# Waiting at the end for all output stores, also for those known to have landed

## The chip, the cores and the metric

The kernel runs on one core of one Trainium2 chip. The metric is the device time of one execution in microseconds (us). The median of three runs of the kernel before is 99.98 us (99.91 to 100.34).

## The reference

The kernel computes one block of linear attention in bf16, with B = 1, S = 2048 rows, D = 640 columns and 32 heads of 20 columns each:

```python
qkv = (x @ wqkv) -> q, k, v, each [B, 32, S, 20]
phi = lambda t: where(t > 0, t + 1, exp(t)) + 1e-6
pq, pk = phi(q), phi(k)
kv = einsum("bhsd,bhse->bhde", pk, v)
z = einsum("bhsd->bhd", pk)
num = einsum("bhqd,bhde->bhqe", pq, kv)
den = einsum("bhqd,bhd->bhq", pq, z) + 1e-6
out = (num / den) @ wo
```

## The kernel before

The rows are cut into 16 tiles of 128, the columns into 5 chunks of 128. The stages overlap, but in the main they follow each other: K for all row tiles and its phi (L293 to L311), the state as a product of x and pk over all rows (L317), Q in blocks of 512 rows and its phi (L354 to L382), the state's product with V's weights and with wo (L445, L472), the denominators (L544) and their inverse, which is multiplied into pq (L569), and at last one product per row tile that gives the output (L576).

No framework orders the work. A small recorder, the class `Plan`, takes each operation with the names that it reads and writes. Each engine has one semaphore and each DMA one of its own. For every operation the recorder computes what it must wait for, and it keeps per engine a clock of what that engine already knows (`known`): the values that it has waited for, and all that the awaited operations knew themselves. A wait that is already known is left out. At the end each engine's list is emitted in the order of recording (`emit`, L78 to L82), SyncE's first. What a wait instruction at L81 is ahead of is the operation at the same place in the list.

The change touches the end. A row tile `st` of the output is evacuated from PSUM into one of four buffers, `osb[st % 4]`, by ScalarE (L599) and VectorE (L602), and `out_dma` (L585 to L590) has SyncE store it with one DMA of 128 x 640. The evacuation into a buffer waits for the store of the tile four earlier, which read the same buffer. The last tile, 15, is cut into four column pieces (`out_last`); SyncE stores its first 480 columns and ScalarE's queue the last 160. So there are 17 stores, 16 of them from SyncE. Each puts a key on `out_keys`.

Behind the lists of all engines, L730 to L734 walk through `out_keys` in order. SyncE gets a wait for each store's semaphore, except where its clock already knows that the store has landed. A wait on a store has the value 16.

```python
for key in out_keys:
    op = P.writers[key]
    if P.known["sp"].get(op.sem, 0) >= op.val:
        continue
    nc.sync.wait_ge(P.sem_obj[op.sem], op.val)
```

Of the kernel before, what the change touches and what calls it, by code (L numbers as in the profile page):

```python
# [84 lines left out]
def bass_standalone__linear_attn_block__prompt_kernel(nc, x, wqkv, wo, out):  # L85
# [15 lines left out]
    with contextlib.ExitStack() as ctx:  # L101
# [38 lines left out]
        P = Plan(nc, es)  # L140
# [588 lines left out]
            P.emit(name, eng)  # L729
        for key in out_keys:  # L730
            op = P.writers[key]
            if P.known["sp"].get(op.sem, 0) >= op.val:
                continue
            nc.sync.wait_ge(P.sem_obj[op.sem], op.val)  # L734


# [26 lines left out]
```

## Time and profile before

| what | value |
|---|---|
| median of three runs | 99.98 us (99.91 to 100.34) |
| the profiled execution | 100.18 us |
| its span, from the first instruction's start to the last one's end | 98.48 us |
| around the span | 1.70 us |
| granted TensorE clock, mean | 1.0 |
| TensorE busy in the span | 95.4 us (97%) |
| last matmul's group on the chain ends | 96.51 us |
| output stores | 15 of 160 KB, one of 120 KB, one of 40 KB |

The profile is of one execution. The span runs from the first instruction to the end of the last one, and the profiled execution's own time is 1.70 us longer; what lies in that difference is not listed by engine. Busy times are per engine, the chain of work is followed back from the last instruction, and a line that begins with SPq or ACTq is about an instruction that SyncE or ScalarE issues for a queue or a wait. L followed by a number is a line of the kernel's source. Instructions that only wait for semaphores (EVENT_SEMAPHORE) are not counted as busy.

### The profile page before, as it was taken

The numbers are of one execution on the slowest core, as the hardware profiler recorded it, in microseconds if no ns is written. First come the engines' busy times: TensorE is split into PE (matmuls) and PEld (weight loads), VectorE is DVE, ScalarE is ACT, GpSimd is POOL, SyncE is SP. The second block draws the span as 40 slices with busy tenths as digits, with TensorE's granted clock in tenths as the row PEclk, the third lists the DMA queues.
The fourth block names the chain that finished last, engine by engine and source line by source line (L and its number), as shares of the span: only waits on it lengthen the run. The fifth ranks groups of instructions, "written<-read, shape, count | busy, mean of one in ns | idle before, by whom it ended". The sixth has DMA issues, their size and how long they took to land.

```text
span 98.5 us, 1813 instructions
## 1 busy us (share of the span) xinstructions
PE 95.4 (97%) x699; PEld 61.1 (62%) x699; DVE 63.7 (65%) x124; ACT 48.8 (50%) x93; POOL 4.7 (5%) x19
## 2 busy tenths in 40 slices
PE   6999999999999999999999999999999999999991
PEld 2567677777755454445587867655557677777771
DVE  5315988988899529997829836758999207272122
ACT  5116455544526220005806466796988765453532
POOL 6400000000000000000000420000000000000000
DMA  2999999999999177000250023313200335632334
GB/s 69 310 258 164 148 222 187 248 379 370 338 163 136 14 169 166 0 0 0 57 83 7 0 61 92 96 29 87 82 0 0 133 72 156 212 122 88 130 133 133
DMA packets 26367, 12.59 MB, mean 128 GB/s; under 512 B 18552, under 2 KB 26360, under 8 KB 26360
## 3 DMA queue, kind: packets, MB, share of 16 engines
q1 hardware_dynamic: 25640, 11.87, 50.3%
q10 hardware_dynamic: 720, 0.61, 1.9%
q8 instruction: 5, 0.08, 0.3%
q14 instruction: 2, 0.02, 0.1%
HBM read 5.90 MB, written 2.62 MB: 87 GB/s over the span
## 4 chain that ended last, share of the span: by engine, by line
PE 93%; DMA 3%; SPq 0%; issue 0%; ACT 0%
PE ps L293 23%; PE ps L576 22%; PE ps L317 22%; PE ps L354 22%; DMA wk<-in_wqkv_dram 3%; PE ps L445 1%; PE ps L544 1%; PE ps L472 1%; SPq L241 0%; PE ps L200 0%; ACT osb L599 0%
## 5 line engine op out<-in xcount | busy, mean ns | idle before, releaser
L317 PE MATMUL ps<-pk,xn 128*128 128x480 bf16 (+1 forms) x160 | 23.2, 299 | 0.0
L354 PE MATMUL ps<-xT,wqn 128*128 128x512 bf16 x100 | 23.1, 379 | 0.0
L293 PE MATMUL ps<-wk,xT 128*128 128x320 bf16 x160 | 22.6, 301 | 0.3 <-DMA wk<-in_wqkv_dram 0.2
L576 PE MATMUL ps<-w2p,pq 128*128 128x320 bf16 (+2 forms) x170 | 22.1, 291 | 0.0
L293 PEld LDWEIGHTS ps<-wk,xT 128*128 128x128 bf16 x160 | 15.5, 98 | 7.2 <-DMA wk<-in_wqkv_dram 0.8
L576 PEld LDWEIGHTS ps<-w2p,pq 128*128 128x128 bf16 x170 | 15.9, 98 | 6.2 <-issue 0.2
L317 PEld LDWEIGHTS ps<-pk,xn 128*128 128x128 bf16 x160 | 13.6, 98 | 9.4 <-issue 0.3
L362 ACT ACTIVATE eq<-ps 128x512 bf16<-128x512 f32 x20 | 11.9, 597 | 13.8 <-PE ps L354 13.6
L354 PEld LDWEIGHTS ps<-xT,wqn 128*128 128x128 bf16 x100 | 11.5, 118 | 9.1 <-issue 0.3
L306 ACT ACTIVATE ek<-ps 128x640 bf16<-128x640 f32 x16 | 11.2, 704 | 11.0 <-PE ps L293 10.3
L599 ACT CAST osb<-ps 128x320 bf16<-128x320 f32 (+2 forms) x27 | 11.0, 413 | 9.7 <-PE ps L576 8.8
L311 DVE SCALAR_TENSOR_TENSOR pk<-ps,ek 128x640 bf16<-128x640 f32 x16 | 13.2, 825 | 0.6
L569 DVE TENSOR_TENSOR pq<-pq,rd 128x512 bf16<-128x512 bf16 x20 | 7.3, 418 | 4.3 <-DMA rd<-rdc 4.3
L375 DVE TENSOR_SCALAR eq<-eq 128x512 bf16<-128x512 bf16 x20 | 5.7, 287 | 5.9 <-ACT eq L362 5.8
L602 DVE CAST osb<-ps 128x320 bf16<-128x320 f32 (+1 forms) x7 | 3.2, 455 | 8.7 <-PE ps L576 8.7
L308 DVE TENSOR_SCALAR ek<-ek 128x640 bf16<-128x640 bf16 x16 | 5.2, 325 | 5.3 <-ACT ek L306 5.3
L366 ACT ACTIVATE rq<-ps 128x512 bf16<-128x512 f32 x13 | 7.7, 592 | 0.0
L339 ACT CAST pt<-ps 128x480 bf16<-128x480 f32 x4 | 2.3, 563 | 8.2 <-PE ps L317 8.1
L379 DVE TENSOR_TENSOR pq<-eq,rq 128x512 bf16<-128x512 bf16 x13 | 5.5, 425 | 1.1 <-ACT rq L366 0.7
L388 DVE TENSOR_TENSOR za<-pk 128x1280 f32<-128x1280 bf16 x4 | 5.8, 1483 | 0.0
L382 DVE SCALAR_TENSOR_TENSOR pq<-ps,eq 128x512 bf16<-128x512 f32 x7 | 4.8, 692 | 0.2
L388 DVE TENSOR_TENSOR za<-za 128x1280 f32<-128x1280 f32 x3 | 4.4, 1487 | 0.0
(37 smaller groups left out, 36.6 us busy)
## 6 DMA issues: line engine op xcount, KB each, us to landing
out_dram<-osb SPq DMA_DIRECT2D x15, 160.0 KB, 1.8
xn<-in_x_dram SPq DMA_DIRECT2D x2, 640.0 KB, 9.3
xn<-in_x_dram SPq DMA_DIRECT2D x1, 960.0 KB, 7.4
wqn<-in_wqkv_dram SPq DMA_DIRECT2D x1, 800.0 KB, 5.3
wv<-in_wqkv_dram SPq DMA_DIRECT2D x5, 150.0 KB, 4.6
wog<-in_wo_dram SPq DMA_DIRECT2D x2, 375.0 KB, 5.0
w2p<-w2g SPq DMA_DIRECT2D x10, 75.0 KB
rd<-rdc SPq DMA_DIRECT2D x8, 64.0 KB, 2.2
```

The lines of the kernel that those rows point to most:

```text
L293: r = e.matmul(bank(b + h, HALF), xT[:, c * S + 128 * st:c * S + 128 * st + 128], wk[:, c * D + HALF * h:c * D + HALF * (h + 1)], start=(c ...
L306: P.add("act", lambda e: e.activation(fold(t[:, :]), two_banks(b), ACTF.Exp), reads=banks + ["table"], writes=[("ek", st % 3)])
L311: P.add("dve", lambda e: e.scalar_tensor_tensor(fold(pk[:, st * D:(st + 1) * D]), two_banks(b), 0.0, fold(t[:, :]), ALU.max, ALU.add), rea ...
L317: return e.matmul(bank(d // PB[h], PW[h], off=PW[h] * (d % PB[h])), xn[:, st * D + 128 * d:st * D + 128 * d + 128], pk[:, st * D + PO[h]:s ...
L354: r = e.matmul(bank(b), wqn[:, d * D:(d + 1) * D].rearrange("p (q c) -> p c q", c=NC_)[:, c, :], xT[:, d * S + BK * sbk:d * S + BK * (sbk ...
L362: P.add("act", lambda e: e.activation(t[:, :], bank(b), ACTF.Exp), reads=[("bank", b), "table"], writes=[("eq", i)])
L366: P.add("act", lambda e: e.activation(r[:, :], bank(b), ACTF.Relu), reads=[("bank", b), "table"], writes=[("rq", i)])
L375: P.add("dve", lambda e: e.tensor_scalar(t[:, :], t[:, :], 1.0, 1e-6, ALU.min, ALU.add), reads=[("eq", i)], writes=[("eq", i)])
L388: P.add("dve", lambda e: e.tensor_tensor(d_ap, a, b, ALU.add), reads=ra + rb, writes=[dst])
L569: P.add("dve", lambda e: e.tensor_tensor(v, v, rd[i][:, BK * h:BK * (h + 1)], ALU.mult), reads=[("rd", i, 2 * h), ("rd", i, 2 * h + 1), (" ...
L576: r = e.matmul(bank(b, hi - lo), pq[:, c * S + 128 * st:c * S + 128 * st + 128], w2p[:, c * D + lo:c * D + hi], start=(c == 0), stop=(c == ...
L599: P.add("act", lambda e: e.copy(osb[j][:, lo:hi], bank(b, hi - lo)), reads=[("bank", b)], writes=keys)
```

## The change

The test is taken out, so that SyncE waits for the store of every row tile in the order of `out_keys`, 17 waits in all.

```diff
         for key in out_keys:
             op = P.writers[key]
-            if P.known["sp"].get(op.sem, 0) >= op.val:
-                continue
             nc.sync.wait_ge(P.sem_obj[op.sem], op.val)
```

## Prediction

> **What bounds the kernel now.** I read the profile in this order: the busy times and the 40 slices, the chain that ended last, then the end of the span alone: SyncE's waits, the last stores, and the wait instructions themselves.
>
> First the page's head and its chain (engine, busy time, share of the span, count; then shares by engine and by line).
>
> ```profile
> PE 95.4 (97%) x699; PEld 61.1 (62%) x699; DVE 63.7 (65%) x124; ACT 48.8 (50%) x93; POOL 4.7 (5%) x19
> ...
> PE 93%; DMA 3%; SPq 0%; issue 0%; ACT 0%
> PE ps L293 23%; PE ps L576 22%; PE ps L317 22%; PE ps L354 22%; DMA wk<-in_wqkv_dram 3%; PE ps L445 1%; PE ps L544 1%; PE ps L472 1%; SPq L241 0%; PE ps L200 0%; ACT osb L599 0%
> ```
>
> The reader is to see that TensorE sets the time up to the last output matmul. SyncE appears with 0%. The change touches no engine but SyncE, and SyncE only behind its last store. So the only stretch that can change is the one from there to the end, and what follows the span.
>
> That stretch is shown by three views. The timeline of the queues' issues at the end (start, length, queue, line):
>
> ```profile
> 96.54 0.33 SPq L587 DMA_DIRECT2D out_dram<-osb  x1
> ```
>
> ```profile
> 96.84 0.35 ACTq L587 DMA_DIRECT2D out_dram<-osb  x1
> ```
>
> The output stores, from their issue to their landing:
>
> ```profile
> L587 SPq DMA_DIRECT2D out_dram<-osb x16: 332/333/1278, 75.8 to 96.5; - x16
> L587 ACTq DMA_DIRECT2D out_dram<-osb x1: 353/353/353, 96.8 to 96.8; - x1
> ...
> DMA to landing us min/median/max: 1.6/1.8/3.1
> ```
>
> And SyncE's waits at the end, first as instructions (duration ns min/median/max, start of the first and the last), then as time waited (total, times, longest):
>
> ```profile
> L734 SPq EVENT_SEMAPHORE  x3: 17/28/28, 97.5 to 98.5; - x3
> ```
>
> ```profile
> SPq L734 <- DMA out_dram<-osb: 1.4, 2, 0.8
> ```
>
> SyncE finishes issuing tile 15's first 480 columns at 96.54 + 0.33 = 96.87 us. ScalarE issues the last 160 columns at 96.84, and they land 1.6 us later, at 98.44 by the trace's landing events. The span ends at 98.48. So SyncE stands idle from 96.87 to the end but for three wait instructions, and what ends last is a landing, not an instruction of SyncE. By the trace the last wait starts 17 ns after the last landing (98.453 after 98.436) and takes 28 ns, which gives 98.481.
>
> **What the change adds.** Before, the loop at L730 to L734 leaves out every store whose landing SyncE already knows: tile t's evacuation into one of the four osb buffers waited for the store of tile t-4, and SyncE's store of tile t waited for that evacuation, so SyncE's clock knows the stores of tiles 0 to 11. Five waits remain: tiles 12, 13, 14, and tile 15 twice. The trace holds them in three instructions, since two waits share one: by their semaphores (14), (15 first part, 13), (15 last part, 12). Without the test there are 17 waits. The built programs, laid side by side, have nine wait instructions there instead of three, and nothing else differs on any engine: (8), (9, 7), (10, 6), (11, 5), (12, 4), (13, 3), (14, 2), (15 first part, 1), (15 last part, 0). So the change adds six instructions on SyncE. It removes nothing, moves no DMA and passes no queue.
>
> Nothing is queued behind these waits on SyncE but its end, and no other engine waits for SyncE there. The first six instructions wait for stores 3 to 13 alone. Store 13 was complete at 96.05 us, before SyncE gets to them, so all six go through at once. The seventh waits for store 14 (97.45), the eighth for the first part of 15 (98.27), the ninth for its last part (98.44). These three are the same three landings as before. The already known halves of the pairs cost no wait.
>
> **The price of a wait that is already met** is not in this place of the trace, because every one of the three waits there had to wait or followed one that did. The nearest rows are SyncE's ten wait instructions at L81, 17 ns each by the view of that line, ahead of its DMAs. In four of the ten, the next DMA on SyncE starts 47 ns after the wait does, in one 65. In five it starts 747 ns after, but there the DMA itself also waits for VectorE's copy, which ends later, so 747 ns is not the wait's own. The bounds for one added instruction are thus 17 ns from below and 65 ns from above, with 747 ns as the end farthest off, excluded as a price for that reason. Pairs took 28 ns where a single wait took 17, so I add 11 ns to the 47 and take 58 ns. A negative price is excluded: the end can't come before the last landing at 98.436, so the most that could be won is 17 + 28 = 45 ns, or 0.05%.
>
> Sum on the profiled run: six instructions at 58 ns are 0.35 us; SyncE passes them from 96.87 to 97.22. The seventh is ready before its landing at 97.45, with 0.23 us to spare. At 65 ns it is 97.26, at 17 ns 96.97. All of it lies beside the flight of the last two stores. If the cover were gone, that is, if these stores landed at once, the change would cost its 0.35 us, or 0.35%. On the path that sets the end it adds 0.00 us: span 98.48, profiled run 100.18 as before, with 1.70 us around the span. The profiled run stands 0.20 us above the median of the three runs (99.98), inside their spread (99.91 to 100.34), so I carry the change of zero over to the median: **99.98 us**.
>
> [...]
>
> **The rivals.**
>
> **The waits outlast the flight (slower).** SyncE has 98.436 - 96.873 = 1.56 us for the eight instructions ahead of the last; from 0.195 us for each they decide the end. For it speaks only that a met wait on a DMA's semaphore isn't in the trace by itself. Against it stand four gaps of 47 ns, a third of that or less. At 0.26 us each, for instance, the last would start at 96.87 + 8 x 0.26 = 98.95 and the time would be some 0.5 us longer, 100.5 us. At the excluded 747 ns it would be 102.85, some 4.4 us longer. Chance 0.03.
>
> **SyncE's instructions no longer fit what is loaded (slower, the other side).** The page lists instruction transfers of their own in the span:
>
> ```profile
> q8 instruction: 5, 0.08, 0.3%
> q14 instruction: 2, 0.02, 0.1%
> ```
>
> The two on q14 (8 KB each) start at 48.03 and 49.64 us and take 0.34 and 0.54 us. The trace has one more of 8 KB at 99.62 us, behind the span, which took 0.34 us. So some engine goes on to new code after the kernel's end. SyncE runs 78 instructions before and 84 after. If the six push SyncE over the edge of a block at a point where nothing hides the transfer, that is, behind 98.48, the time grows by one transfer: 0.34 to 0.54 us, or 100.32 to 100.52 us. Inside the span it would be hidden as the waits are, by 1.56 us of flight. It decides from the first instruction past the edge. Against it: six instructions are few, and the trace shows no stall of TensorE at its own transfers on q8. The upper end is slower by over 0.5%, the lower isn't. Chance 0.10: 0.04 at the lower price (two of the three rows) and 0.06 at the dearer, with which go the 16 KB transfers on q8, 0.88 to 1.18 us each by the trace, should SyncE's be of their kind.
>
> **The change doesn't do what it says.** If the added waits were folded away, SyncE would still show three wait instructions, and the time would be 99.98 as well. The nine instructions in the built program speak against it. Chance 0.01.
>
> **Faster.** The mechanism's limit is 45 ns. What remains is drift between the chips on which medians are taken; the runs shown lie as far as 0.36 us from their median. A median 0.5 us lower lies beyond all of them: about 99.4. Chance 0.03.
>
> **How the numbers follow.** Hidden as forecast: 0.79. With the third rival's 0.01 and the 0.04 of the cheap transfer, within 0.5% has 0.84. Slower by over 0.5% (100.48 and up) has the first rival's 0.03, the dear transfer's 0.06, 0.02 for drift upward and 0.01 for what I haven't thought of: 0.12. Faster by over 0.5% (below 99.48) has its 0.03 and such a hundredth too: 0.04. The bound of 0.5% is about what a measurement of this kernel can tell from no change. The range reaches down by the farthest run's distance, 99.98 - 0.36 = 99.62, and up to the dearer 8 KB transfer, 99.98 + 0.54 = 100.52. Outside it lie the first rival, the drifts and a transfer of the q8 kind, about a tenth in all.
>
> **What would show it.** Right: nine wait instructions at the loop's line in the place of three, six of them in a row between 96.9 and 97.3 at 17 to 28 ns each, some 50 to 60 ns apart; the last landing at about 98.4 and the span's end within 50 ns behind it. Wrong: a last wait that starts later than about 20 ns after the last landing (the first rival); a third q14 transfer in the span, or an unchanged span with a longer execution around it (the second); three wait instructions (the third). My forecast would also be wrong if SyncE's busy waiting delayed the landings themselves: then the stores' 1.6 us to landing would grow.

## The result and the profile after

Over 22 runs of each, the kernel after took 99.56 us (99.19 to 100.34) and the kernel before 100.19 us (99.72 to 102.76). The ratio is 0.9954, with a 95% interval of 0.9938 to 0.9970. The change is a gain of about 0.46 us (0.30 to 0.62). The forecast was no change, 99.98 us in a range from 99.62; the result lies below that range. Some executions of several kernels, of before too, took over 1.5% longer than the fastest (102.76 us here); the ratios and the averages below leave them out.

The page after, its head and the chain that ended last:

```profile
span 98.3 us, 1814 instructions
...
PE 95.1 (97%) x694; PEld 61.2 (62%) x699; DVE 63.7 (65%) x124; ACT 48.8 (50%) x93; POOL 4.7 (5%) x19
...
PE 95%; ACT 2%; issue 0%
```

TensorE still sets the time up to the last output matmul (five matmul records are missing here). What follows is, at first sight, the same end. The output stores of the kernel after, by their view, and its wait instructions (duration ns min/median/max, starts of the first and the last):

```profile
L587 SPq DMA_DIRECT2D out_dram<-osb x16: 332/333/1202, 75.6 to 96.4; - x16
L587 ACTq DMA_DIRECT2D out_dram<-osb x1: 355/355/355, 96.7 to 96.7; - x1
...
DMA to landing us min/median/max: 1.6/1.8/3.0
```

```profile
L732 SPq EVENT_SEMAPHORE  x9: 17/28/28, 96.8 to 98.3; - x9
```

The last store of SyncE, and what its waits at L732 waited for (total, times, longest):

```profile
96.36 0.33 SPq L587 DMA_DIRECT2D out_dram<-osb  x1
```

```profile
SPq L732 <- DMA out_dram<-osb: 0.5, 1, 0.5
```

There are nine wait instructions instead of three, as forecast, and they waited 0.5 us for stores in place of 1.4. From the last matmul's end to the end of the span it takes 1.98 us in both profiled executions, and the last landing comes 1.94 us after that matmul in both. The span of the profiled execution is 0.18 us shorter (98.30 against 98.48), but that is in place already at the last matmul (96.32 against 96.50): it comes from the start, where K's first matmuls on the chain begin at 4.20 us after and at 4.37 before. Before, the chain waits for a load of the K weights until 4.32 us, and such loads vary: the one on the chain took 3.09 us there and 5.39 us in early7, one of the kernels below. Over the 22 runs after, the span alone goes from 97.9 to 99.1 us.

The difference that doesn't vary lies **outside the span**. The profiled execution after took 99.56 us, 1.26 around its span; before it was 1.70. Over all runs with both numbers, time less span averages 1.68 us before (31 runs of one comparison; 1.67 and 1.69 in the two others) and 1.27 us after (22 runs). That is 0.41 us, nearly the whole gain.

Two views show what moved. First the code transfers and stores at the end, before and then after, in 40 slices of 0.125 us from 96 to 101 us (upper row the busy share of the DMA engines in tenths, lower row GB/s):

```profile
DMA  0000899710079996000000000000100000000000
GB/s 0 0 0 10 287 348 358 277 31 0 23 246 330 300 264 141 8 0 0 0 0 0 0 0 0 0 0 0 66 0 0 0 0 0 0 0 0 0 0 0
```

```profile
DMA  0029994003999930010000000000000000000000
GB/s 0 0 82 358 358 358 154 0 0 100 300 330 290 223 69 0 0 66 0 0 0 0 0 0 0 0 0 0 0 0 0 0 0 0 0 0 0 0 0 0
```

The lone 66 behind the two humps of the last stores is 8 KB of code on q14. By the records it starts at 99.62 us before, 1.14 us after the span's end, and at 98.17 us after, 0.13 us ahead of the span's end. The page after counts it within the span, where the page before had two such transfers of 8 KB (the other added record is one of 40 bytes at the start):

```profile
q14 instruction: 4, 0.02, 0.1%
```

Second, the wait instructions of the kernel after, in three windows, 96.7 to 97.2, 97.2 to 98 and 98 to 99 us:

```profile
L732 SPq EVENT_SEMAPHORE  x4: 17/28/28, 96.8 to 97.0; - x4
```

```profile
L732 SPq EVENT_SEMAPHORE  x3: 28/28/28, 97.4 to 97.6; - x3
```

```profile
L732 SPq EVENT_SEMAPHORE  x2: 28/28/28, 98.1 to 98.3; - x2
```

The first four start 65 to 70 ns apart (96.751, 96.816, 96.886, 96.956). The fifth starts only at 97.438, although it waits for the stores of tiles 12 and 4, which had landed at 94.56 at the latest. Nothing that the profile shows held it. SyncE **stopped for 0.41 us** beyond its step of 0.07, behind its 79th instruction. 1.19 us after the stop began (96.984, the end of the 79th), the code transfer starts. Before, SyncE's program had 78 instructions, so if the place is fixed, this stop came behind the last wait, in the time around the span, with nothing to hide it. No view shows the stop itself there; the experiments are to tell.

### The profile page after: what moved, and what is told of

Its sections match the earlier page's. It is cut to its first block, busy times and chain, and to the rows that moved or that the text cites. A ratio compares the mean times of both kernels' runs of the same rounds, so it can differ in the third digit from the quotient of the medians.

```text
span 98.3 us, 1814 instructions
## 1 busy us (share of the span) xinstructions
PE 95.1 (97%) x694; PEld 61.2 (62%) x699; DVE 63.7 (65%) x124; ACT 48.8 (50%) x93; POOL 4.7 (5%) x19
## 3 DMA queue, kind: packets, MB, share of 16 engines
HBM read 5.90 MB, written 2.62 MB: 87 GB/s over the span
## 4 chain that ended last, share of the span: by engine, by line
PE 95%; ACT 2%; issue 0%
PE ps L293 23%; PE ps L576 22%; PE ps L354 22%; PE ps L317 21%; PE ps L283 3%; ACT w2g L483 2%; PE ps L445 1%; PE ps L544 1%; PE ps L200 1%; PE ps L472 1%; ACT osb L599 0%
## 5 line engine op out<-in xcount | busy, mean ns | idle before, releaser
L354 PE MATMUL ps<-xT,wqn 128*128 128x512 bf16 x95 | 22.0, 379 | 0.4 <-issue 0.2
```

The costliest lines, as they stand in the source:

```text
L354: r = e.matmul(bank(b), wqn[:, d * D:(d + 1) * D].rearrange("p (q c) -> p c q", c=NC_)[:, c, :], xT[:, d * S + BK * sbk:d * S + BK * (sbk ...
```

## The experiments

Theory A: SyncE's stream has a stop of 0.41 us at a fixed place, behind its 79th instruction, followed some 1.1 us later by a transfer of 8 KB of code. What counts is where the stop falls: behind the last wait it lengthens the time, beside the flight of the last stores it is free. Rival B: waits that are already met, at the end, save time by themselves, in proportion to their number. Rival C: drift in the loads.

In the table, "after the stop" is how many of SyncE's instructions come behind the stop; "tail" is the time from the last matmul's end to the span's end in the profiled execution; "around" is the mean of time less span over the runs; "code" is when the 8 KB transfer starts, counted from the last matmul's end.

| kernel | waits at the end | SyncE instructions | after the stop | tail us | around us | code us | ratio to before, 95% |
|---|---|---|---|---|---|---|---|
| before | 5 | 78 | none | 1.98 | 1.68 | 3.13 | |
| after | 17 | 84 | 5 | 1.98 | 1.27 | 1.85 | 0.9954 (0.9938 to 0.9970) |
| plus1 | 7 | 79 | none | 1.99 | 1.78 | 3.06 | 1.0016 (0.9995 to 1.0038) |
| plus2 | 9 | 80 | 1 | 2.30 | 1.29 | 2.89 | 0.9994 (0.9977 to 1.0012) |
| plus3 | 11 | 81 | 2 | 1.99 | 1.25 | 2.16 | 0.9947 (0.9928 to 0.9966) |
| merged15 | 15 | 79 | none | 1.98 | 1.79 | 3.06 | 0.9993 (0.9955 to 1.0030) |
| early4 | 5 | 82 | 3 | 2.08 | 1.25 | 1.66 | 0.9952 (0.9924 to 0.9980) |
| early5 | 5 | 83 | 4 | 2.85 | 1.28 | 1.10 | 1.0038 (1.0006 to 1.0071) |
| early5_again | 5 | 83 | 4 | 2.62 | 1.26 | 1.10 | one run |
| early6 | 5 | 84 | 5 | 2.21 | 1.25 | 0.59 | 0.9980 (0.9952 to 1.0008) |
| early6_again | 5 | 84 | 5 | 2.09 | 1.23 | 0.60 | 0.9950 (0.9924 to 0.9976) |
| early7 | 5 | 85 | 6 | 1.99 | 1.26 | -0.47 | 0.9968 (0.9944 to 0.9992) |

The column "code" moves with the 79th instruction: in each of the eleven profiled executions that have one, the transfer starts 1.06 to 1.27 us after that instruction's end, wherever it stands, even where the stop itself is hidden under a wait (plus3, early4, early6, early7) or lies behind the span (plus1, merged15).

### Fewer added waits at the end: plus1, plus2, plus3

The loop leaves out all but the last two, four or six of the twelve known stores (10 stands for 10, 8 and 6):

```diff
-        for key in out_keys:
+        for at, key in enumerate(out_keys):
             op = P.writers[key]
-            if P.known["sp"].get(op.sem, 0) >= op.val:
+            if at < 10:
                 continue
```

> Seven waits at the end, one instruction more on SyncE than before (79). Theory A (SyncE's stream has a fixed stop of about 0.41 us behind its 79th instruction; before, it falls behind the last wait and lengthens the time around the span): the stop still lies behind the last wait. Around the span 1.70 us as before, time as before within 0.1 us. Rival B (each wait at the end that is already met saves a share of the 0.44 us by itself, in proportion to the six): around the span 1.63 us, time 0.07 us less. Rival C (the gain is drift in the early loads): around the span the same in all kernels.

> Nine waits, two instructions more than before (80). Theory A: the stop falls between the wait for tile 15's first part and the last wait. That wait begins about 0.41 us after the one ahead of it is met, some 0.3 us later than before: span 98.8 us, around it 1.26 us, time 0.1 us less than before. Rival B: around the span 1.55 us, the span unchanged, time 0.15 us less.

> Eleven waits, three instructions more than before (81). Theory A: the stop falls between the wait for tile 14 and the wait for tile 15's first part, beside the stores' flight, and is hidden whole: span 98.5, around it 1.26 us, time 0.44 us less than before, as much as with all six. Rival B: half of the gain, around the span 1.48 us, time 0.22 us less.

One more instruction gains nothing: around the span 1.78 us, 0.1 more than before and more than theory A's 1.70. Two move the stop in between the last two waits: the time around the span drops to 1.29 us and the tail grows by 0.31, and the sum can't be told from before. The wait instructions of plus2 in the windows 98.13 to 98.5 us and 98.5 to 99.5 us; the first is the wait for tile 15's first part, which starts at 98.12 and reaches into its window, the second the last wait:

```profile
L734 SPq EVENT_SEMAPHORE  x1: 28/28/28, 98.1 to 98.1; - x1
```

```profile
L734 SPq EVENT_SEMAPHORE  x1: 27/27/27, 98.6 to 98.6; - x1
```

They start 0.48 us apart (98.119 and 98.599), although the last landing came at 98.27 in between: 0.41 us beyond the step of 0.07.

Three instructions more bring the whole gain at once: 0.9947, around the span 1.25. It is a step, not a line. Rival B would have given 0.07, 0.15 and 0.22 us.

### The same number of instructions, elsewhere: early6 and early4

The loop at the end is that of before. Waits on input loads are put ahead of SyncE's transpose of z (L423), where SyncE is idle for 13 us; two of them share an instruction. Twelve waits make six instructions; early4 has eight, which make four:

```diff
                     reads=[("zh", "zl")[i]], writes=[("zt", i)], dma=True)
+            first = P.ops["sp"][-2]
+            first.waits = [(f"d:{k}", 16) for k in range(12)] + first.waits
```

> The end as before the change (five waits); twelve waits on loads that have long landed stand ahead of the transpose of the sums z, where SyncE is idle for 13 us: 84 instructions as after the change. Theory A: the stop comes ahead of the last store, where SyncE waits 0.5 us for its data anyway: span 98.5, around it 1.26 us, time 0.44 us less than before although the end is untouched. Rival B: nothing, around the span 1.70 us, time as before.

> The end with five waits as before; eight waits on landed loads ahead of the transpose of z make four instructions more on SyncE (82). Theory A (a stop of 0.41 us behind SyncE's 79th instruction): the stop falls right behind SyncE's last store, ahead of the wait for tile 14, and lies beside that store's flight: span 98.4, around it 1.26 us, time 0.44 us less than before. Rival B (met waits at the end save time by themselves): around the span 1.70, time as before.

early4 gains as much as the change, 0.9952, with an untouched end. The stop lies between the last store's issue and the wait for tile 14. Rival B falls: it expected nothing. In early6 the time around the span is 1.25 us as theory A has it, but the ratio, 0.9980, holds no clear gain, and the tail was 2.21 us. In that profiled execution the last matmul already ended 2.4 us later than in the one before (98.91 against 96.50 us), so only its end is read here. A second set of runs follows.

> The kernel with six early instructions once more, for an undisturbed look at its end. Theory A: around the span 1.26 us; the stop lies beside the 0.5 us for which SyncE waits for tile 15's data, so the last store is issued at most 0.05 us later than before and the span is 98.5 us. If the span comes out 0.2 us or more longer again, the stop, or the transfer of code behind it, isn't hidden in this place, and the trace should show the last store issued or landed later against the last matmul.

This time it gains 0.50% (0.9950), but the tail is still 0.11 us longer than before. SyncE's last store was issued 0.074 us after the last matmul, 0.03 later than before, and landed 0.09 later. What ends the span is ScalarE's store: issued in time, it landed 0.11 us late. In early4 it landed 0.09 us late too, which is that kernel's longer tail (2.08 us).

### Many waits, but no more instructions: merged15

Fifteen waits stay at the end, eight instructions. The five loads of 10 KB for V's last group become one, so that SyncE has four instructions fewer elsewhere, and 79 in all. The loop at the end is that of plus1 with 2 in the place of 10; the other part of the edit:

```diff
+                if n == 1:
+                    P.add("sp", lambda e, g=g, f=f: e.dma_start(
+                        wv[:, :].rearrange("p (d j f) -> p d j f", d=NC_, f=64)[:, :, 2 * g, 0:f],
+                        wqkv[:, 2 * D + goff[g]:2 * D + goff[g] + f].rearrange("(d p) f -> p d f", p=128)),
+                        writes=[("wv", g, d) for d in range(NC_)], dma=True)
+                    continue
```

> Fifteen waits at the end (eight wait instructions, five more than before), but the five small loads of V's last group (128 x 40 each) are one DMA, so that SyncE has four instructions fewer elsewhere: 79 in all, as with seven waits. Theory A: the stop falls behind the last wait again and the gain is gone: around the span 1.70 to 1.78 us, time as before within 0.1 us. Rival B: most of the gain stays (five of six instructions), around the span 1.33 us, time 0.37 us less.

The gain is gone, with most of the added waits in place: 0.9993, and 1.79 us around the span. The code transfer is behind the span again, 3.06 us after the last matmul; in 40 slices of 0.125 us from 96 to 101 us (the span ends at 98.79):

```profile
GB/s 0 0 0 0 0 0 123 358 358 348 123 0 0 123 315 330 274 223 46 0 0 0 0 0 0 0 0 0 0 0 66 0 0 0 0 0 0 0 0 0
```

This runs against rival B as plainly as early4 does. Rival C falls with both, since the time around the span, where no load lies, is 1.67 to 1.79 us in every kernel with at most 79 instructions on SyncE and 1.23 to 1.29 in every kernel with 80 or more.

### The stop on the path: early5, and early7

Ten early waits, five instructions, put the stop right ahead of SyncE's last store; fourteen, seven instructions, put it ahead of tile 14's store. The edit is that of early6 with 10 and 14.

> As the kernel with four early instructions, but with five (83). Theory A: the stop falls between the wait for the last tile's data and the last store of SyncE, on the path: that store is issued and lands 0.4 us later than before, which ends after ScalarE's store: span 98.7, around it 1.26 us, time 0.2 us less than before only, and 0.24 us more than with one early instruction fewer. Rival B: nothing.

In early5 the stop is where theory A puts it. The last stores' issues, ScalarE's and SyncE's:

```profile
96.75 0.38 ACTq L589 DMA_DIRECT2D out_dram<-osb  x1
```

```profile
96.86 0.33 SPq L589 DMA_DIRECT2D out_dram<-osb  x1
```

SyncE's last store starts 0.466 us behind the wait ahead of it, where before the step was 0.047: 0.42 us of stop. But the sum was wrong: 0.38% slower instead of 0.2 us faster. Against the last matmul, the issue came 0.42 us later than before and the landing 0.97. ScalarE's store, issued in time (0.35 us after the last matmul, as before), landed 0.54 us late too. The view of the stores in the window of the last two shows it, where the kernel after has 1.6/1.7/1.7 in the same window:

```profile
DMA to landing us min/median/max: 2.1/2.2/2.3
```

The transfers from 96 to 100.8 us, in slices of 0.12, show what stands ahead of them:

```profile
GB/s 0 0 0 181 352 352 352 128 0 0 0 0 68 48 256 328 312 262 112 16 24 8 0 0 0 0 0 0 0 0 0 0 0 0 0 0 0 0 0 0
```

The 68 is the code transfer, 1.10 us after the last matmul and now ahead of the data of both stores, in their flight. It took 0.60 us, and the tail of the second hump is drawn out (16, 24, 8). The tail of 2.85 us, 0.87 longer than before, outweighs the 0.40 us that leave the time around the span.

> The kernel with five early instructions once more, one look. Theory A with a held-up landing: the last store of SyncE is issued 0.42 us later against the last matmul than before, and since the code transfer falls into the flight, both last stores land about 0.5 us later than the issue alone would say: 2.6 to 2.9 us from the last matmul to the end. If the first look's extra 0.5 us was chance, 2.4 us.

The second run has a tail of 2.62 us, ScalarE's landing 0.34 us late and SyncE's 0.31 beyond its later issue: smaller, but again late, with a transfer of 0.50 us.

> Five waits at the end, fourteen waits (seven instructions) ahead of the transpose of z, 85 instructions on SyncE. Theory A: the stop of 0.41 us stands between the wait for tile 14's first piece of data and tile 14's store, which comes 0.75 us later anyway, so it is hidden. The code transfer that follows about 1.1 us behind the stop starts near 96.1 us and is over before the last two stores move data. If that transfer is what held up the landings in the kernels with five and six early instructions, the landings are free of it: 1.98 us from the last matmul to the end of the span as before, around it 1.26 us, time 0.44 us less than before. If instead the early waits themselves made the end longer, it stays at 2.08 to 2.2 us.

early7 has the most early waits, and its tail is back at 1.99 us, with landings as before to 10 ns. So the early waits by themselves don't lengthen the end. Its code transfer started 0.47 us ahead of the last matmul's end and was over before the last two stores moved data; in its slices from 96 to 100.8 us the 68 stands by itself ahead of two clean humps:

```profile
GB/s 0 0 75 299 341 352 278 22 0 0 68 0 0 0 75 309 395 352 224 11 0 24 232 328 331 256 179 16 0 0 0 0 0 0 0 0 0 0 0 0
```

Its ratio, 0.9968, is a gain of 0.32 us, where 0.44 was expected; 0.44 us (0.9956) lies inside its interval, so the shortfall isn't shown. If it is real, it lies ahead of the last matmul, since the time around the span is 1.26 and the tail as before; whether seven early instructions have a share in it stays open.

## Why the prediction was wrong

**What bounds the kernel, and the added instructions: right.** Nine wait instructions in place of three, six more on SyncE, and no other engine changed. A met wait took 65 to 83 ns after, apart from the stop (59 to 95 in merged15), where 58 was the value taken and 65 the upper bound; that the bound was too low cost nothing beside the flight. The waits lie beside the stores' flight, and the last landings stayed at 1.94 us after the last matmul. Within the span the sum of zero was right.

**The step that failed** is the sentence "profiled run 100.18 as before, with 1.70 us around the span". It took the 1.70 us for a constant that the kernel's text can't touch, and gave no reason for that. 0.41 us of it was SyncE's stop, which six more instructions pulled ahead of the end: the time around the span measured 1.27 us after, and 1.79 with eight wait instructions but 79 instructions in all. For the same reason "the most that could be won is 17 + 28 = 45 ns" was wrong: that bounds the end of the span, not of the execution.

**The rival that came closest had the wrong sign and the wrong price.** It asked whether the six instructions would push SyncE over the edge of a block of code behind the span, and would have priced that at one more transfer, 0.34 to 0.54 us. A fixed place was there, but the kernel before already paid for it behind the span: the transfer at 99.62 us, which the prediction quoted, fits it, 1.14 us after the span's end. With the place fixed, adding instructions could only move the stop forward, into cover that the same prediction had measured at 1.56 us. Nor is the transfer's own length the price. SyncE goes on at 97.44 us after, 0.73 us before the transfer starts, so the stop isn't a wait for that transfer to land; it is 0.41 us by the gap in the waits and by the time around the span, before against after, alike.

**The waits outlast the flight: rightly set aside.** The first eight left the ninth free in time: it began at 98.276, 16 ns after the last landing.

**The second wait of a pair: priced too high.** The prediction added 11 ns for a second wait in an instruction. After, the step was 65 ns from an instruction with one wait and 70 from three of the four met ones with two (83 from the other), so a second wait added 5 ns in most of them.

What stays open: what SyncE does during the 0.41 us, and why the time around the span is 0.10 us longer when the stop comes straight behind the last wait (1.78 and 1.79 us) than one instruction later (1.68). Whether the stop is the edge of a block of code, as the rival had it, no run shows.

## What to carry to other kernels

In this case the engine that was the last to finish paid in full for a stop in its instruction stream that came after the last thing it waited for (0.41 us by the time around the span, before against after); a handful of harmless instructions ahead of it, or a few fewer, moved that stop under a wait or out of it (around the span 1.27 us after, 1.79 in merged15). So when a small edit on one engine changes the time by some tenths of a us and the span doesn't account for it, compare the time around the span, count that engine's instructions, and look for the code transfer on the instruction queue. Here the time around the span wasn't a constant: 1.23 to 1.79 us, by that engine's instructions alone.

## What the runs showed of the hardware

- SyncE stopped for about 0.41 us behind its 79th instruction in each kernel where the place could be seen: 0.41 us in the kernel after and in plus2, 0.42 in early5, 0.43 in its repeat. By the time around the span it was 0.41 us before (1.68 against 1.27) and 0.51 where it came straight behind the last wait (1.78 and 1.79).
- The transfer of 8 KB of code starts 1.06 to 1.27 us after the 79th instruction ends, in all eleven profiled executions that have one (plus1 1.06, plus2 1.07, early5 1.08, after 1.19, early4 1.27).
- Where that transfer fell into the flight of the last stores, these landed later than their issue explains, by 0.06 to 0.55 us (early5 and early5_again most, both runs of early6, and one store of early4). Where it ran well before or behind, they kept to 10 ns of the kernel before (plus1, plus2, plus3, merged15, early7), and in the kernel after too, where it starts 0.09 us ahead of the last landing. That the transfer holds the stores up is the likeliest reading; no run moved it without the stop.
- In early5 and its repeat, a store issued 0.42 to 0.43 us later thus landed 0.75 to 0.97 us later.
